# Column sums of w_out on VectorE instead of TensorE, with a new order of every engine's queue, in a clustered-attention and feed-forward kernel

## The chip, the cores and the metric

The kernel runs on one core of one Trainium2 chip. The metric is the device time of one execution in microseconds (us); the time before is the median of 3 runs, 220.64 us (220.5 to 221.01).

## The reference

Clustered attention (4 batches, 8 heads, 768 tokens, head dimension 64, 16 clusters) is followed by a feed-forward layer with a SoLU, a layer norm without bias and a second product (3072 tokens, d_model 512, d_ff 1024). All inputs and the output are float32.

```python
q_assign = argmax(q_n @ c_n.T); k_assign = argmax(k_n @ c_n.T)      # normalised rows, 16 clusters
scores = scale * q @ k.T, kept where q_assign == k_assign, else -1e9
x = softmax(scores) @ v                                              # -> (3072, 512)
h = x @ w_in
solu = h * exp(h - max(h)) / sum(exp(h - max(h)))
ln = (solu - mean(solu)) / sqrt(var(solu) + 1e-6) * g_ln
out = ln @ w_out
```

## The kernel before, in words

**The work.** The attention is cut into 96 units of 256 queries against 768 keys (24 per batch). The scores of all units are one long row of columns, cut into 144 regions of 1024. For region r, `S{r}.0` and `S{r}.1` are TensorE products into one of two PSUM tiles `sb` (L644), `E{r}` is the exponential on ScalarE (L654), and `V{n}.0`, `V{n}.1` are the products of unit n with the values, into the PSUM tile `ob` (L666). Units are put in groups; in batch 0 group g is units 2g and 2g+1. `N{g}` on VectorE divides the group by its sums (a reciprocal, L678, and a product, L689) and so empties `ob`: the first V of group g+1 needs N{g} (L1154 to L1158). Batch 0 has regions S0 to S35.

**Its operands.** In batches 1 to 3 the loads `ld` (L412, four pieces of 192 KB for two pairs of heads, read in runs of 32 floats, 128 bytes) fill the tiles `raw`; `xt` (L420, VectorE) transposes them; `ca` (L436 to L440) casts them, mostly on GpSimd, into `qbig` and `kbig`; `cl` (L469, TensorE) multiplies with the cluster centres, and `tb`, `mx`, `oh`, `ot` (VectorE) and `pl` (L541) turn that into cluster rows of `qbig` and `kbig`. `lv` (L558) loads the values, `cv` casts them. `ld1.0.0` is the q and `ld1.0.1` the k of batch 1's first two pairs, `ld1.2.0` the q of the next two. `cl1.0` needs `xt1.0.0` and `xt1.0.1`.

**The feed-forward part.** Row tiles of 128 tokens, f = 0 to 23, run in between: `h` (L777), `hm`, `ex`, `u`, `tu`, `bn`, `y` (L849), `sc`, `ou`. The layer norm's mean is folded into the weights: `w_out_c` is g·w_out less the mean of g·w_out over d_ff. `lo0` to `lo3` load w_out, two blocks of 128 rows each, into `w_g` (L599, 512 KB); `li0` and `li1` load w_in with a cast to bfloat16 from GpSimd's queue (L583). `gk` keeps -g as `g_ln2`. `gw` (L595, GpSimd) spreads g/d_ff over 32 columns in `g_wide`; `me0` and `me1` (L605, TensorE) sum the columns of w_out with it in eight float32 products, each of which is two instructions in the profile, 32 rows of PSUM to each product of four; `mk` (L614, VectorE) copies the sums out; `mf` (L617, two instructions) adds the four strips with the constant matrix `fold` and spreads the mean to 128 rows; `km` (L614) copies it out; `ce0` to `ce7` (L621 on VectorE, L625 with L627 on GpSimd) make `w_out_c`. `y0.0` needs `ce0` and `ce1`.

**What sets the order.** Every step is a named entry; `ORDER` lists all of them by hand, and each engine runs its own in that order, each waiting for what it reads. `AWAY` moves a step to another engine. SyncE's (SP's) queue issues nearly all loads, and one hardware queue (q1 in the profile) serves them. GpSimd's loads are on a software queue (q0). Both use the same 16 DMA engines.

Of the kernel before, what the change touches and what calls it, by code (L numbers as in the profile page):

```python
# [38 lines left out]
lc ld0.0.0.0 ld0.0.1.0 ld0.0.0 ld0.0.1 wu ld0.1.0 ld0.1.1 ld0.2.0 cx cy lv0.0 ld0.2.1 tp0.0.0.0 cz  # L39
ld0.3.0 tp0.0.0.1 xa0.0.0 lg tp0.0.1.0 xt0.0.0 ca0.0.0.0.0 lv0.1 cp lo1 ca0.0.0.0.1 cb tp0.0.1.1  # L40
xa0.0.1 ld0.3.1 ca0.0.0.1.0 ca0.0.1.0.0 cl0.0 cc lo2 xt0.0.1 ca0.0.0.1.1 tp0.1.0.0 tb0.0
ca0.0.1.1.0 tp0.1.0.1 mx0.0 xa0.1.0 cl0.0.1 ca0.0.1.0.1 oh0.0 xt0.1.0 tp0.1.1.0 ca0.0.1.1.1 tb0.0.1
ld1.0.0.0 tp0.1.1.1 xa0.1.1 ca0.1.0.0 mx0.0.1 ot0.0 ld1.0.0.1 xt0.1.1 tp0.2.0.0 oh0.0.1 pl0.0.1.1
tp0.2.0.1 xa0.2.0 ot0.0.1 cl0.1 z1 pl0.0.1.0 pl0.0.0.1 pl0.0.0.0 cv0.0.0 pl0.0.1.1.0 xt0.2.0 S0.0
pl0.0.1.0.1 S0.1 pl0.0.1.1.1 tb0.1 tp0.2.1.0 pl0.0.1.0.0 E0 S1.0 xa0.2.1 tp0.2.1.1 ca0.1.0.1 S1.1
xt0.2.1 cv0.0.1 tp0.3.0.0 ca0.2.0.0 S2.0 E1 mx0.1 S2.1 cl0.2 z4 oh0.1 ca0.2.1.0 E2 xa0.3.0 S3.0
S3.1 ot0.1 V0.0 tp0.3.0.1 E3 ca0.1.1.0 S4.0 S4.1 xt0.3.0 V0.1 ca0.2.1.1 V1.0 E4 V1.1 tb0.2 S5.0 lo0
S5.1 z2 pl0.1.1.1 N0 tp0.3.1.0 E5 S6.0 pl0.1.1.0 xa0.3.1 S6.1 V2.0 lo3 V2.1 mx0.2 pl0.1.0.1 E6
tp0.3.1.1 ld1.0.0.2 pl0.1.0.0 S7.0 ca0.1.1.1 gt xt0.3.1 S7.1 lv0.2 cv0.1.1 V3.0 V3.1 gk oh0.2 S8.0
# [2 lines left out]
pl0.2.1.1 V6.0 V6.1 oh0.3 ca0.3.0.1 S12.0 S12.1 ca0.3.1.0 V7.0 S13.0 E12 ld1.0.1.1 S13.1 ot0.3
ca0.3.1.1 cv0.2.0 me1 E13 pl0.3.0.0 S14.0 pl0.3.1.0 cv0.2.1 lv0.3 S14.1 mk V7.1 E14 pl0.3.1.1 S15.0
N3 S15.1 mf z3 ld1.0.1.2 pl0.3.0.1 E15 ld1.0.1 S16.0 km S16.1 V8.0 V8.1 E16 li0 S17.0 ce2 S17.1
V9.0 V9.1 E17 S18.0 N4 S18.1 li1 ld1.2.0.0 E18 S19.0 S19.1 cv0.3.0 cv0.3.1 xt1.0.0 ld1.2.0.1 E19
V10.0 V10.1 ce1 V11.0 V11.1 S20.0 N5 S20.1 S21.0 E20 S21.1 V12.0 V12.1 xt1.0.1 E21 V13.0 S22.0
S22.1 ce3 ca1.0.1.0 V13.1 E22 S23.0 N6 S23.1 cl1.0 xt1.1.0 E23 ce0 S24.0 S24.1 ptx0 xt1.1.1 V14.0
V14.1 E24 V15.0 S25.0 S25.1 tx0 V15.1 E25 z5 ca1.1.0.0 S26.0 N7 S26.1 cl1.1 ce5 E26 tb1.1 S27.0
S27.1 tb1.0 V16.0 V16.1 E27 S28.0 mx1.0 S28.1 V17.0 V17.1 ld1.2.0.2 E28 ca1.0.0.0 S29.0 N8 S29.1
h0.0.0 oh1.0 E29 V18.0 ld1.2.0 S30.0 S30.1 h0.0.1 ot1.0 E30 S31.0 S31.1 ld1.2.1.0 V18.1 ce4 V19.0  # L60
E31 pl1.0.0.0 V19.1 S32.0 S32.1 N9 h0.1.0 ld1.2.1.1 E32 hm0.0 S33.0 pl1.0.1.1 S33.1 V20.0 h0.1.1
E33 ld1.2.1.2 pl1.0.1.0 S34.0 S34.1 V20.1 V21.0 E34 V21.1 pl1.0.0.1 S35.0 ld1.2.1 N10 S35.1 h1.0.0
E35 ca1.0.1.1 hm0.1 S36.0 S36.1 lv1.0 V22.0 xt1.2.0 h1.0.1 bl1.0 E36 S37.0 S37.1 hm1.0 ca1.0.0.1
V22.1 tx2 V23.0 E37 V23.1 S38.0 N11 S38.1 ca1.1.1.0 h1.1.0 E38 lv1.1 S39.0 ca1.2.0.0 S39.1 h1.1.1
tx4 E39 xt1.2.1 S40.0 ca1.1.1.1 S40.1 E40 hm1.1 cl1.2 xt1.3.0 cv1.0.0 ex0.0 S41.0 S41.1 cv1.0.1
V24.0 V24.1 tb1.2 V25.0 V25.1 E41 V26.0 u0.0 S42.0 V26.1 S42.1 N12 h2.0.0 E42 h2.0.1 xt1.3.1 V27.0
h2.1.0 ex1.0 ce6 tu0 S43.0 hm2.0 S43.1 h2.1.1 E43 V27.1 S44.0 hm2.1 ld2.0.0.0 S44.1 h3.0.0 E44
ld2.0.0.1 bn0.0 cl1.3 u1.0 bn0.1 lv1.2 ex2.0 V28.0 V28.1 tb1.3 S45.0 V29.0 V29.1 mx1.2 ld2.0.0.2
S45.1 h3.0.1 ca1.2.1.0 E45 ld2.0.0 S46.0 S46.1 oh1.2 h3.1.0 ca1.3.0.1 E46 y0.0 N13 h3.1.1 cv1.1.1
S47.0 S47.1 bn1.0 ca1.1.0.1 cv1.1.0 ld2.0.1.0 y0.1 E47 hm3.0 S48.0 S48.1 y0.2 ot1.2 E48 tu1 V30.0  # L70
S49.0 S49.1 ce7 V30.1 V31.0 E49 V31.1 ld2.0.1.1 S50.0 as0 as1 ca1.2.0.1 pl1.2.0.1 bn1.1 S50.1
h4.0.0 ld2.0.1.2 E50 hm3.1 S51.0 pl1.2.1.1 S51.1 V32.0 ag0 V32.1 E51 y0.3 pl1.2.1.0 N14 S52.0 S52.1
h4.0.1 ld2.0.1 pl1.2.0.0 al0 E52 S53.0 as2 S53.1 bl1.2 V33.0 u2.0 V33.1 E53 h4.1.0 lv1.3 hm4.0
h4.1.1 ag1 ex3.0 V34.0 S54.0 xt2.0.0 ld2.2.0.0 S54.1 S55.0 S55.1 ld2.2.0.1 ca1.2.1.1 V34.1 E54 sc0
V35.0 h5.0.0 u3.0 h5.0.1 hm4.1 E55 S56.0 S56.1 bn2.0 y1.0 E56 bn2.1 S57.0 ld2.2.0.2 S57.1 V35.1
hm5.0 y1.1 cv1.2.0 ca2.0.0.1 y1.2 E57 N15 tu2 S58.0 ca2.0.0.0 S58.1 xt2.0.1 h5.1.0 E58 al1 S59.0
S59.1 ou0 xt2.1.0 V36.0 ca1.3.1.0 V36.1 ld2.2.0 V37.0 V37.1 E59 V38.0 ld2.2.1.0 cv1.2.1 ag2 S60.0
S60.1 ca1.3.0.0 xt2.1.1 h5.1.1 E60 V38.1 y1.3 as3 hm5.1 cv1.3.0 S61.0 ex4.0 S61.1 ca1.3.1.1 S62.0
bn3.0 ld2.2.1.1 S62.1 cl2.1 N16 al2 E61 cl2.0 u4.0 bn3.1 tu3 E62 sc1 V39.0 V39.1 S63.0 tb2.1 S63.1
# [1279 lines left out]
```

## Time and profile before

| | |
|---|---|
| median of 3 runs | 220.64 us |
| profiled execution, first to last instruction | 224.4 us |
| TensorE (PE) busy | 213.4 us, 95% |
| ScalarE (ACT) busy | 190.0 us, 85% |
| VectorE (DVE) busy | 182.4 us, 81% |
| GpSimd (POOL) busy | 162.3 us, 72% |
| mean granted TensorE clock | 0.992 |

The profile is of one execution of its own. It gives a span of 224.4 us, 3.8 us over the median of the timed runs, and no other time of its own; differences worked out in the profile are taken over to the median as they are. In a timeline row the numbers are start, duration, engine, line, operation, tiles and shape, with the idle time before it and what ended that in brackets. A row of stretches gives the busy time of each engine in the stretch (instructions in parentheses), then the granted clock, the mean busy share of the DMA engines and GB/s. SPq is SyncE's issuing of a DMA.

### The profile page before, as it was taken

To read this page: it belongs to the slowest core of one execution; us is meant where nothing else is said; L and a number is where in the kernel's file an instruction comes from. 1 tells how busy PE (TensorE), PEld (TensorE's weight loads), DVE (VectorE), ACT (ScalarE), POOL (GpSimd) and SP (SyncE) were. 2 spreads that over 40 slices of the span, in tenths; PEclk is the share of its full clock that TensorE was granted. 3 is DMA by queue.
4 is the path that set the end of the run, shared out by engine and by line. 5 is a ranking of instruction groups with operands and counts; after the bars stand their busy time and mean duration, and the time that the engine had idled before them with its cause. 6 is when DMAs were issued, how large, how long until landed. Compare 5 with 4: busy or idle time off the path is not lost.

```text
span 224.4 us, 6272 instructions
## 1 busy us (share of the span) xinstructions
PE 213.4 (95%) x2400; PEld 149.4 (67%) x2431; DVE 182.4 (81%) x431; ACT 190.0 (85%) x239; POOL 162.3 (72%) x202
## 2 busy tenths in 40 slices
...
GB/s 212 386 350 225 171 179 201 170 174 104 50 75 179 149 184 212 181 214 177 216 147 275 164 157 102 169 116 173 113 209 96 94 34 165 133 167 128 189 61 142
DMA packets 120878, 37.28 MB, mean 166 GB/s; under 512 B 109960, under 2 KB 116368, under 8 KB 120848
## 3 DMA queue, kind: packets, MB, share of 16 engines
...
HBM read 23.11 MB, written 6.29 MB: 131 GB/s over the span
## 4 chain that ended last, share of the span: by engine, by line
PE 81%; POOL 8%; DMA 4%; DVE 2%; issue 2%; SPq 0%; DVEq 0%; POOLq 0%
PE sb L644 24%; PE hb L777 17%; PE mb L849 16%; PE ob L666 13%; PE hb L469 5%; DMA raw<-in_k_dram 4%; POOL kbig L440 2%; POOL qbig L438 2%; PE hb L849 2%; PE sb L952 1%; POOL kbig L541 1%; POOL v L566 1%; POOL qbig L541 1%; PE hb L395 1%; DVE cst L483 0%
## 5 line engine op out<-in xcount | busy, mean ns | idle before, releaser
L654 ACT ACTIVATE e<-sb 128x1024 bf16<-128x1024 f32 x144 | 140.0, 1022 | 16.5 <-PE sb L644 15.2
L644 PE MATMUL sb<-qbig,kbig 80*128 80x256 bf16 (+3 forms) x648 | 85.3, 262 | 0.7 <-ACT e L654 0.3
L644 PEld LDWEIGHTS <-kbig 80*128 80x128 bf16 (+1 forms) x648 | 62.4, 120 | 25.3 <-issue 8.2
L810 POOL TENSOR_TENSOR u<-e_sb,w_st 128x1024 bf16<-128x1024 bf16 x21 | 45.1, 2147 | 18.7 <-ACT e_sb L803 12.3
L666 PEld LDWEIGHTS <-e 128*128 128x128 bf16 x1152 | 48.8, 98 | 12.3 <-issue 1.9
L666 PE MATMUL ob<-v,e 128*128 128x65 bf16 x1140 | 51.9, 193 | 0.4 <-DVE x L689 0.2
L777 PE MATMUL hb<-w_in_sb,xT 128*128 128x512 bf16 x172 | 50.4, 379 | 0.6
L849 PE MATMUL mb<-w_out_c,uT 128*128 128x512 bf16 x157 | 43.6, 379 | 0.6
L821 DVE BATCH_NORM_STATS2 bs<-u 128x6 f32<-128x512 bf16 x48 | 31.8, 681 | 1.1 <-POOL u L810 1.1
L803 ACT ACTIVATE e_sb<-w_st,nmax 128x1024 bf16<-128x1024 f32 (+1 forms) x25 | 27.9, 1114 | 5.5 <-DVE w_st L787 4.1
L440 POOL TENSOR_SCALAR kbig<-xt 64x768 bf16<-64x768 f32 (+1 forms) x30 | 27.4, 916 | 6.8 <-DVE xt L420 5.3
L438 POOL CAST qbig<-xt 64x768 bf16<-64x768 f32 (+1 forms) x32 | 26.7, 837 | 5.8 <-DVE xt L420 2.1
L420 DVE STREAM_TRANSPOSE xt<-raw 128x768 f32<-128x768 f32 x24 | 22.6, 961 | 5.3 <-DMA raw<-in_k_dram 5.2
L845 POOL TENSOR_TENSOR alpha<-var,halves 128x1 f32<-128x1 f32 x24 | 15.8, 659 | 11.8 <-DVE var L828 11.2
L849 PEld LDWEIGHTS <-uT 128*128 128x128 bf16 x176 | 15.2, 97 | 9.6
L777 PEld LDWEIGHTS <-xT 128*128 128x128 bf16 x192 | 16.1, 98 | 7.9
L787 DVE TENSOR_SCALAR_CACHE_REDUCE w_st<-hb,nmax 128x512 f32<-128x512 f32 x24 | 17.8, 743 | 3.2 <-PE hb L777 2.6
L689 DVE TENSOR_TENSOR x<-ob,den 128x256 bf16<-128x256 f32 (+2 forms) x40 | 19.0, 474 | 1.4
L787 DVE TENSOR_SCALAR_CACHE_REDUCE w_st<-hb 128x512 f32<-128x512 f32 x24 | 16.3, 679 | 4.1 <-PE hb L777 4.1
L678 DVE RECIPROCAL den<-ob 128x4 f32<-128x4 f32 (+2 forms) x40 | 7.2, 180 | 10.1 <-PE ob L666 9.6
L469 PE MATMUL hb<-xt,c_bd 128*32 128x384 f32 x96 | 11.4, 522 | 3.3 <-DVE xt L420 3.3
L541 POOL COPY qbig<-oht 32x768 f32<-32x768 f32 (+2 forms) x11 | 9.1, 824 | 6.5 <-DVE oht L508 3.3
...
## 6 DMA issues: line engine op xcount, KB each, us to landing
...
```

Of the source, the lines that this page charges most:

```text
L438: (nc.vector if e == "DVE" else nc.gpsimd).tensor_copy(dst, src)
L440: (nc.vector if e == "DVE" else nc.gpsimd).tensor_scalar(dst, src, scalar1=inv_C, scalar2=1.0, op0=Alu.mult, op1=Alu.mult)
L469: nc.tensor.matmul(bank_of(t, n)[c * NB:(c + 1) * NB, :L], w, xts[b, p, i][:, c0 + x * L:c0 + (x + 1) * L] .rearrange("p (n q) -> p q n", ...
L644: nc.tensor.matmul(reg[:, c:c + wd], kb[u, pp, side_of(h), keys], qb[u, pp, side_of(h), su * P:su * P + wd])
L654: nc.scalar.activation(es[r][:, :w], src, Act.Exp, scale=exp_scale, bias=-exp_scale)
L666: nc.tensor.matmul(ops_of(group_of[n])[:, s, :VW], es[r][:, c0:c0 + P], v1[index[b, pair_of(h)] % R][:, side_of(h), kt, :VW], start=(kt == ...
L777: nc.tensor.matmul(hb[f2][:], xTs[f][:, dc, :], w_in_sb[:, dc, f2 * BANK:(f2 + 1) * BANK], start=(dc == 0), stop=(dc == n_dc - 1))
L787: nc.vector.tensor_scalar(ff[f, "h"][:, f2 * BANK:(f2 + 1) * BANK], hb[f2][:], scalar1=-1.0, scalar2=nmax[:, f2 - 1:f2] if f2 else 3.0e38, ...
L803: nc.scalar.activation(ff[f, "e"][:, cols(f, f2)], ff[f, "h"][:, cols(f, f2)], Act.Exp, bias=ff[f, "nmax"][:, n_ff2 - 1:], scale=-1.0, acc ...
L810: (nc.vector if e == "DVE" else nc.gpsimd).tensor_tensor(ff[f, "u"][:, cols(f, f2)], ff[f, "e"][:, cols(f, f2)], ff[f, "h"][:, cols(f, f2) ...
L821: nc.vector.bn_stats(ff[f, "bs"][:, f2, :], ff[f, "u"][:, f2 * BANK:(f2 + 1) * BANK])
L849: nc.tensor.matmul(y_of(f, x), ff[f, "uT"][:, fc, :], w_out_c[:, fc, parts_of(f, x)], start=(fc == 0), stop=(fc == n_fc - 1))
```

## The change

- `me0` to `me7` are now VectorE operations, one for each block of 128 rows of w_out: the first multiplies block 0 with -g into the float32 tile `part`, the others multiply block fc with -g and add it to `part`. `me{fc}` needs `lo{fc // 2}`. `gw` and `mk` are gone, and `mf` sums `part` over all 128 rows with a `fold` of 1/d_ff.
- `cc` (which fills `c_bd`) is now needed only by the `cl` of batches 1 to 3, and the first `h` and `ptx0` no longer wait for `mk` or `km`.
- `ORDER` is another for every engine. SP now issues `lo2` alone early; `lo0` stands between the pieces of `ld1.0.1`, `lo3` and `lo1` behind it.
- In the new `ORDER`, `me2` stands ahead of `N5` on VectorE, and `N5` ahead of `V12.0` on TensorE; `cl1.0` stands ahead of `S22.0` (before: ahead of `S24.0`). `mf` stands behind `E34`, `km` behind `E35` (before: behind `S15` and `S16.0`).

```diff
@@ AWAY, to DVE
-    ce2 ce4 cv0.3.0 km mk pl0.0.0.0 pl0.1.0.0 pl0.2.0.1 pl0.2.1.0 pl0.3.0.0 pl1.2.0.0 pl2.0.0.0
+    ce2 ce4 cv0.3.0 km pl0.0.0.0 pl0.1.0.0 pl0.2.0.1 pl0.2.1.0 pl0.3.0.0 pl1.2.0.0 pl2.0.0.0
...
@@ ORDER (one line of each)
-S10.1 tb0.3 V5.0 ld1.0.0 V5.1 E10 sg S11.0 pl0.2.1.0 ld1.0.1.0 ca0.2.0.1 S11.1 N2 me0 E11 mx0.3
+E19 li1 ld1.2.0 S20.0 xt1.1.0 V11.1 S20.1 cv0.3.1 E20 me2 S21.0 ld1.2.1.0 S21.1 z5 cl1.0 N5 E21
...
-    def widen_g():
-        nc.gpsimd.tensor_scalar(g_wide[:], g_ln2[:].unsqueeze(2).to_broadcast([P, n_fc, NB]),
-                                scalar1=1.0 / d_ff, scalar2=1.0, op0=Alu.mult, op1=Alu.mult)
...
-    def sum_w_out(x):
-        for c in range(4):
-            fc = 4 * x + c
-            nc.tensor.matmul(hb[1][c * NB:(c + 1) * NB, :], g_wide[:, fc, :], w_g[:, fc, :],
-                             start=(x == 0), stop=(x == n_fc // 4 - 1),
-                             tile_position=(0, c * NB))
+    def sum_w_out(fc):
+        if fc == 0:
+            wt["part"] = mo.tile([P, d_model], F32, name="y")
+            nc.vector.tensor_scalar(wt["part"][:], w_g[:, fc, :], scalar1=g_ln2[:, fc:fc + 1],
+                                    scalar2=None, op0=Alu.mult)
+            return
+        nc.vector.scalar_tensor_tensor(out=wt["part"][:], in0=w_g[:, fc, :],
+                                       scalar=g_ln2[:, fc:fc + 1], in1=wt["part"][:],
+                                       op0=Alu.mult, op1=Alu.add)
...
-                [f"{half}{b}.{p}.0", f"{half}{b}.{p}.1", "cb"]
+                [f"{half}{b}.{p}.0", f"{half}{b}.{p}.1", "cb" if early(b) else "cc"]
...
-            add("ptx0", "PE", 0.46, s, turn_x_first, nd + hb_free[1][-1:] + ["mk"], take="h1")
+            add("ptx0", "PE", 0.46, s, turn_x_first, nd + hb_free[1][-1:], take="h1")
...
-                    nd += hb_free[f2][-1:] + ["mk" if f2 else "km"]
+                    nd += hb_free[f2][-1:]
...
-    add("sg", "POOL", 0.26, 8, lambda: nc.gpsimd.memset(fold[:], 1.0 / NB), ["cp"])
-    for x in range(2):
-        add(f"me{x}", "PE", 0.9, 16 + x, (lambda x=x: sum_w_out(x)),
-            [f"lo{2 * x}", f"lo{2 * x + 1}", "gw"] + ([] if x else hb_free[1][-1:]),
-            ["me0"] if x else list(last_tp), take=None if x else "h1")
-    e = on("mk", "ACT")
-    add("mk", e, 0.55, 18, (lambda e=e: keep("part", 1, e)), ["me1"], give="h1")
-    add("mf", "PE", 0.87, 18, fold_sums, ["mk", "sg"] + hb_free[0][-1:], take="h0")
+    add("sg", "POOL", 0.26, 8, lambda: nc.gpsimd.memset(fold[:], 1.0 / d_ff), ["cp"])
+    for fc in range(n_fc):
+        add(f"me{fc}", "DVE", 0.66, 16 + fc, (lambda fc=fc: sum_w_out(fc)),
+            [f"lo{fc // 2}", "gk"] + ([f"me{fc - 1}"] if fc else []))
+    add("mf", "PE", 0.87, 18, fold_sums, [f"me{n_fc - 1}", "sg"] + hb_free[0][-1:], take="h0")
```

SP's queue before, from the load `lo2` on (the tile `raw_234` is `ld1.0.0`, `raw_508` is `ld1.0.1`, `raw_651` is `ld1.2.0`; `w_g` rows are `lo2`, then `lo0` and `lo3`; `lo1` stands further up):

```order
L599 DMA w_g_110<-in_moe_w_out_dram 128x2x512
L412 DMA raw_234<-in_q_dram 32x48x32 x2
L599 DMA w_g_110<-in_moe_w_out_dram 128x2x512 x2
L412 DMA raw_234<-in_q_dram 32x48x32
L558 DMA vf_424<-in_v_dram 128x2x384
L412 DMA raw_234<-in_q_dram 32x48x32
L412 DMA raw_508<-in_k_dram 32x48x32 x2
L558 DMA vf_574<-in_v_dram 128x2x384
L412 DMA raw_508<-in_k_dram 32x48x32 x2
L412 DMA raw_651<-in_q_dram 32x48x32 x4
```

The same queue now, from `lo2` on (`raw_229` is `ld1.0.0`, `raw_389` is `ld1.0.1`, `raw_555` is `ld1.2.0`; the `w_g` rows are `lo2`, `lo0`, `lo3`, `lo1`):

```order
L594 DMA w_g_110<-in_moe_w_out_dram 128x2x512
L411 DMA raw_229<-in_q_dram 32x48x32 x2
L557 DMA vf_349<-in_v_dram 128x2x384
L411 DMA raw_389<-in_k_dram 32x48x32
L594 DMA w_g_110<-in_moe_w_out_dram 128x2x512
L411 DMA raw_389<-in_k_dram 32x48x32
L557 DMA vf_455<-in_v_dram 128x2x384
L411 DMA raw_389<-in_k_dram 32x48x32 x2
L594 DMA w_g_110<-in_moe_w_out_dram 128x2x512
L411 DMA raw_555<-in_q_dram 32x48x32
L594 DMA w_g_110<-in_moe_w_out_dram 128x2x512
L411 DMA raw_555<-in_q_dram 32x48x32
```

All four pieces of `ld1.0.1` stood behind the four loads of w_out; now two of these stand behind them, and the last, `lo1`, also behind the first piece of `ld1.2.0`.

VectorE's queue before, from `N4` on, at the first operands of batch 1 (`N4`, a cast of values, `xt1.0.0`, `N5`, `xt1.0.1`, `ce3`, `N6`, `xt1.1.0` with `xt1.1.1`):

```order
L678 RECIPROCAL den<-ob 128x4 [waits PE_49]
L689 TENSOR_TENSOR x<-ob,den 128x2x2x64 [waits DVE_49]
L566 CAST v_3_105<-vf 128x6x64 [waits DMAHW1_49]
L420 STREAM_TRANSPOSE xt<-raw 128x768 [waits DMAHW6_49,DMAHW4_49,DMAHW0_49]
L678 RECIPROCAL den<-ob 128x4 [waits PE_49]
L689 TENSOR_TENSOR x<-ob,den 128x2x2x64 [waits DVE_49]
L420 STREAM_TRANSPOSE xt<-raw 128x768 [waits DMAHW3_49,DMAHW7_49,DMAHW2_49,DMAHW0_49]
L621 SCALAR_TENSOR_TENSOR w_out_c<-w_g,g_ln_111,y 128x512
L678 RECIPROCAL den<-ob 128x4 [waits PE_49]
L689 TENSOR_TENSOR x<-ob,den 128x2x2x64 [waits DVE_49]
L420 STREAM_TRANSPOSE xt<-raw 128x768 [waits Pool_49] x2
```

The same place now (a cast of values, `xt1.0.0`, `N4`, `me1`, `xt1.0.1`, `xt1.1.0`, `me2`, `N5`, `xt1.1.1`):

```order
L565 CAST v_3_105<-vf 128x6x64 [waits DMAHW7_49]
L419 STREAM_TRANSPOSE xt<-raw 128x768 [waits DMAHW6_49,DMAHW2_49,DMAHW1_49]
L676 RECIPROCAL den<-ob 128x4 [waits PE_49]
L687 TENSOR_TENSOR x<-ob,den 128x2x2x64 [waits DVE_49]
L603 SCALAR_TENSOR_TENSOR y<-w_g,g_ln_111,y 128x512
L419 STREAM_TRANSPOSE xt<-raw 128x768 [waits DMAHW4_49,DMAHW6_49,DMAHW1_49,DMAHW0_49]
L419 STREAM_TRANSPOSE xt<-raw 128x768
L603 SCALAR_TENSOR_TENSOR y<-w_g,g_ln_111,y 128x512 [waits DMAHW4_49,DVE_49]
L676 RECIPROCAL den<-ob 128x4 [waits PE_49]
L687 TENSOR_TENSOR x<-ob,den 128x2x2x64 [waits DVE_49]
L419 STREAM_TRANSPOSE xt<-raw 128x768 [waits Pool_49]
```

`N5` stood ahead of the transpose that waits for `ld1.0.1`; it now stands behind that transpose and behind `me2`, which waits for a load of its own, `lo1`.

More of the change, by code (lines that the diff above doesn't have):

```diff
@@ L38 @@
 ORDER = """
[L39 to L49, printed above, removed]
```

198 lines of the change are left out of this document (103 added, 95 removed).

## The prediction

> **What bounds the kernel now.** The page and the table of stretches come first. The four stretches from 30 to 50 us are cut at the hole that the chain of waits shows; the last three are the rest of the span.
>
> ```profile
> span 224.4 us, 6272 instructions
> core 0: us, PE busy (x) PEld busy (x) DVE busy (x) ACT busy (x) POOL busy (x), PEclk, DMA share, GB/s
> 30.00:37.00 7.00, 6.54 (x96) 4.70 (x92) 3.13 (x8) 6.92 (x8) 4.46 (x6) 1.00 1.15 214
> 37.00:40.40 3.40, 0.13 (x4) 0.06 (x4) 1.09 (x2) 0.54 (x1) 0.02 (x1) 1.00 1.25 205
> 40.40:43.80 3.40, 3.40 (x23) 1.91 (x24) 2.89 (x6) 0.90 (x1) 3.32 (x5) 0.50 0.96 153
> 43.80:50.00 6.20, 6.03 (x88) 4.37 (x87) 4.76 (x10) 5.15 (x7) 3.38 (x4) 1.00 0.95 180
> ...
> 60.00:130.00 70.00, 69.35 (x850) 51.64 (x863) 63.19 (x134) 67.86 (x85) 58.71 (x62) 1.00 1.01 177
> 130.00:200.00 70.00, 69.26 (x798) 49.55 (x811) 56.32 (x140) 62.93 (x80) 48.40 (x51) 1.00 0.66 131
> 200.00:224.40 24.40, 20.56 (x144) 11.13 (x142) 19.26 (x53) 13.10 (x22) 11.04 (x13) 1.00 0.46 135
> ```
>
> From 60 to 200 us TensorE is busy 138.6 of 140 us. So from the end of the hole on, the time is the TensorE work still to be done, and a late restart, or work left over at the restart, goes to the end in full. The hole is 37.0 to 40.4 us: TensorE does 0.13 us of work in it, and the next 3.4 us run at half clock. TensorE's and VectorE's timelines say what ends it.
>
> ```profile
> 34.90 0.60 PE L644 MATMUL sb<-qbig,kbig 80*128 80x256 bf16 x4
> ...
> 36.20 0.87 PE L469 MATMUL hb<-xt,c_bd 128*32 128x384 f32 x4
> 40.34 1.50 PE L469 MATMUL hb<-xt,c_bd 128*32 128x384 f32 x4 [3.27 <-DVE xt L420]
> ...
> 28.04 0.17 DVE L678 RECIPROCAL den<-ob 128x4 f32<-128x4 f32 x1
> 28.25 0.43 DVE L689 TENSOR_TENSOR x<-ob,den 128x256 bf16<-128x256 f32 x1
> ...
> 39.31 0.98 DVE L420 STREAM_TRANSPOSE xt<-raw 128x768 f32<-128x768 f32 x1 [5.25 <-DMA raw<-in_k_dram]
> ```
>
> The first row is S22. `cl1.0` is half done when it waits for `xt1.0.1`, and that waits for the last piece of `ld1.0.1`, to 39.31 us. ScalarE runs dry meanwhile:
>
> ```profile
> 27.84 9.70 ACT L654 ACTIVATE e<-sb 128x1024 bf16<-128x1024 f32 x10 [0.22 <-PE sb L644]
> 42.90 1.02 ACT L654 ACTIVATE e<-sb 128x1024 bf16<-128x1024 f32 x1 [5.37 <-PE sb L644]
> 44.85 15.47 ACT L654 ACTIVATE e<-sb 128x1024 bf16<-128x1024 f32 x16 [0.93 <-PE sb L644]
> ```
>
> The ten end with E23, E24 starts at 42.90 and E25 at 44.85. Why does 192 KB land so late? First, each with its own landing time, the second and third pieces of `ld1.0.1`, the first piece of `ld1.2.0`, `li0` and `li1`; then both DMA queues from 34 to 38 us.
>
> ```profile
> L412 SPq DMA_DIRECT2D raw<-in_k_dram x1: 2446/2446/2446, 24.5 to 24.5; - x1
> DMA to landing us min/median/max: 5.9/5.9/5.9
> ...
> L412 SPq DMA_DIRECT2D raw<-in_k_dram x1: 467/467/467, 29.2 to 29.2; - x1
> DMA to landing us min/median/max: 4.2/4.2/4.2
> ...
> L412 SPq DMA_DIRECT2D raw<-in_q_dram x1: 2162/2162/2162, 30.5 to 30.5; - x1
> DMA to landing us min/median/max: 10.9/10.9/10.9
> ...
> L583 POOL DMA_DIRECT2D w_in_sb<-in_moe_w_in_dram x1: 960/960/960, 30.5 to 30.5; - x1
> DMA to landing us min/median/max: 6.6/6.6/6.6
> ...
> L583 POOL DMA_DIRECT2D w_in_sb<-in_moe_w_in_dram x1: 724/724/724, 31.4 to 31.4; - x1
> DMA to landing us min/median/max: 8.6/8.6/8.6
> ...
> q0 software_dynamic: 393, 0.77, 106.5%
> q1 hardware_dynamic: 244, 0.03, 10.0%
> ```
>
> The second piece lands at 30.4 us, the third at 33.4, the next two only at about 39 and 41.4, because w_in, issued at 30.5 us, takes the engines: in four microseconds its queue moves 0.77 MB and SP's 0.03 MB. The Trainium skill's page "DMA: Bandwidth & Descriptors" (Queues, rings and completion order) states that an engine goes round its queues packet by packet; the trace agrees as far as small packets behind large ones get few bytes.
>
> **Part by part: what is removed.** The sums on TensorE, their copy and the spreading of g:
>
> ```profile
> L605 PE MATMUL hb<-w_g,g_wide 128*32 128x512 f32 x16 | 2.1, 605 | 0.0
> L614 DVE COPY y<-hb 128x512 f32<-128x512 f32 x2 | 1.4, 692 | 0.7 <-PE hb L617 0.7
> L617 PE MATMUL hb<-y,fold 128*128 128x512 f32 x2 | 1.1, 632 | 0.0
> L621 DVE SCALAR_TENSOR_TENSOR w_out_c<-w_g,g_ln,y 128x512 bf16<-128x512 f32 x4 | 3.0, 757 | 0.0
> ```
>
> The sixteen take 2.1 us of TensorE, one copy 0.69 us of VectorE. All of it stands ahead of the hole, and who comes early to a hole waits longer. I cost it at nothing; if the hole were gone, TensorE's 2.1 us would count in full.
>
> **Added.** Eight operations like L621 (0.757 us; same elements, a bfloat16 output there), 6.1 us less the copy, 5.4 us of VectorE. `me0` and `me1` stand ahead of the hole, `me2` in it. `me3` to `me7` come after, 3.8 us; between 60 and 130 us VectorE has 6.8 of 70 us free, so they can be hidden, but not all at once. I take 0 us, with 2 us as the upper end (VectorE or GpSimd late by half of that work, since three GpSimd `ce` also move to where GpSimd is busy 58.7 of 70 us).
>
> **Moved: the loads.** Two prices are needed. A large load runs at the 386 GB/s of the page's second slice, before the small runs begin: 512 KB (524 thousand bytes) in 1.4 us, 384 KB in 1.0.
>
> ```profile
> GB/s 212 386 350 225 171 179 201 170 174 104 50 75 179 149 184 212 181 214 177 216 147 275 164 157 102 169 116 173 113 209 96 94 34 165 133 167 128 189 61 142
> ```
>
> A piece of 192 KB in runs of 128 bytes is 1536 packets: 1.1 us at the rate of SP's queue from 42 to 46 us (first row below), and 2.0 by the landings, since from 30.4 to 33.4 us one piece and one 384 KB load of values came in. I take the middle, 1.55.
>
> ```profile
> q1 hardware_dynamic: 5696, 0.72, 113.1%
> ...
> q0 software_dynamic: 2, 0.00, 2.7%
> ```
>
> (The second row is w_in's queue from 31 to 33 us: it has hardly begun.) Without w_in the last piece of `ld1.0.1` was due at 33.4 + 1.55 = 34.95; it now gets ahead of two of the 512 KB loads, and lands at 34.95 - 2.8 = 32.2, ahead of w_in's packets. That wait is then over.
>
> What is late next is `lo1`. On SP's queue it now stands behind exactly what before stood ahead of, and with, the first piece of `ld1.2.0`: the same set of transfers, in another order, on the same engines. That set was complete at 30.5 + 10.9 = 41.4 us. If w_in is issued at about the same time, 41.4 us is when `lo1` lands. GpSimd's queue holds the same steps ahead of w_in as before, less `gw`.
>
> On VectorE `me2` waits for `lo1`, and behind it are queued `N5`, `xt1.1.1`, `me3`, `N6`. TensorE waits for `N5` at `V12.0`, with S22 done; ScalarE then has nothing after E22. So: 41.4 + 0.76 (`me2`) + 0.64 (`N5`, 28.04 to 28.68 for an equal one) = 42.8 us for TensorE's restart, against 40.34 before: **+2.5 us**. Both restarts are at half clock, at the same price.
>
> **Work left over at the restart.** By the queues, before had done V12, V13, S23, `mf` and half of `cl1.0` when it restarted; now the four V and two S products and `mf` are still to do, and `cl1.0` is done. Prices from the chain of waits:
>
> ```profile
> 44.32 0.44 PE sb L644 x4
> 45.38 0.85 PE hb L469 x8
> 50.55 0.55 PE ob L666 x18
> ```
>
> V: 24 products at 0.55/18, 0.73 us; S23 0.44; `mf` 1.10 (L617); less half a `cl`, 0.42. Sum **+1.85 us**. Together 4.3 us: 224.4 goes to 228.7, the median 220.64 to **224.9**.
>
> A lower bound by ScalarE's pace: at half clock V12, V13 and S23 take 2.3 us, so E23 starts at 45.1 and E25 at 47.1, against 44.85: +2.2, 222.8. The rest of the new order can gain little: from 60 us on TensorE is idle 1.4 us and then 3.8 in the tail, mostly behind its last product. If `lo1` lands at 38 us, caught by part of w_in only, it is 3.4 less than 4.3: 221.5. With the 2 us above, this case reaches from 221.5 to 226.9.
>
> **The rivals.** *`lo1` escapes (faster).* If w_in's packets come after `lo1`, the set is complete at 33.4 plus two pieces: 36.5 us (35.6 to 37.4). `N5` ends at 37.9, the restart is 2.45 us earlier, the work left over still 1.85: -0.6. TensorE's hole is then from 35.3 (S22 done, at 34.90 + 0.44, if it comes when it did) to 37.9. If the clock stays up over so short a hole, half of 3.4 us more is saved: -2.3. I take -1.4, 219.2. It decides at w_in's issue: its packets began 2.5 us after it, at 33 us, so GpSimd would have to issue 3 us later than before, after 33.5. For it speaks that GpSimd waits in its queue for VectorE and TensorE, which have another order; against it, that it has less to do.
>
> The Trainium skill's page "TensorE: Matmul & The Clock Gate" (Part 1) states that the clock halves after an idle window of about 3.4 us. Before, 3.27 us of idleness were followed by 3.4 us at 0.50, so the trace agrees roughly; by that rule a hole of 2.6 us is likely spared.
>
> *The hole vanishes (faster).* With `lo1` ahead of 33.9 us TensorE goes on at 35.3: 5.0 us earlier, less 1.85, and 1.7 of clock: -4.85, 215.8. SP's queue would have to be some 2.6 us faster than by its rates above.
>
> *`lo1` half caught (no change).* Landing near 37.1 us, restart at 38.5: 220.6.
>
> *VectorE and GpSimd over-full (slower).* The late `me` and `ce` push `N`, `hm` and the casts back, and TensorE waits outside the hole: 2 us on top, 226.9. It decides if VectorE has no idle time between 43 and 60 us; before, it was busy 4.76 of 6.20 us at the start of that stretch.
>
> **How the numbers follow.** The forecast, with landings of `lo1` between 38 and 42 us, has 0.56; over-full engines 0.14; `lo1` escapes 0.17; the hole vanishes 0.05; half caught 0.08. A measurement of this kernel can tell 0.2%, 0.44 us, from no change. Faster 0.22, same 0.08, slower 0.70. The range is 218.5 to 227.0: it leaves out the vanished hole, the fast end of the escape and the slow end of the over-full case, about 0.15. The forecast's own range is 221.5 to 226.9.
>
> **What would show it.** VectorE's second in-place SCALAR_TENSOR_TENSOR waits for a DMA of `w_g` to about 41 us; the reciprocal behind it starts near 42; TensorE has a hole from about 35 to 42.8 that VectorE's x ends; E23 starts near 45. `xt1.0.1` runs near 33 us. Wrong would be a landing of `lo1` before w_in's two, a hole under 3 us, or, with the hole as said, a TensorE that is idle much less after it than before.

## The result and the profile after

The changed kernel takes 233.28 us (median of 4 runs, 231.7 to 234.78), the kernel before beside it 220.58 (220.5 to 221.01): a ratio of 1.0552 (95% interval 1.0466 to 1.0639), 12.7 us slower. The forecast was 224.9 us, 4.3 slower. The direction was right, the size three times the forecast, and the time lies above the range (227.0).

The times of the changed kernel and of its variants scatter by 2 to 10 us from run to run, those of the kernel before by 1.5; the ratios leave out runs more than 1.5% above the fastest of their kernel (in run 5 four of six), the medians keep them.

The page of the changed kernel, and what TensorE waited for in it:

```profile
span 233.0 us, 6274 instructions
...
PE 217.4 (93%) x2415; PEld 150.8 (65%) x2415; DVE 190.8 (82%) x438; ACT 191.0 (82%) x239; POOL 159.7 (69%) x201
...
PEclk9999985599999999999999999999999999999999
...
engine line waited for: us in total, times, longest us
PE ob L664 <- DVE x L687: 5.3, 3, 2.9
PE hb L775 <- DVE cst L482: 2.0, 1, 2.0
```

Two of the waits for x stand close together, and TensorE's timeline and VectorE's show them (line 603 is `me1` to `me7`, lines 676 and 687 are `N`, 565 is `cv0.3.0`, 419 is `xt`):

```profile
32.90 0.49 PE L664 MATMUL ob<-v,e 128*128 128x65 bf16 x6 [2.25 <-DVE x L687]
42.22 1.48 PE L664 MATMUL ob<-v,e 128*128 128x65 bf16 x24 [2.88 <-DVE x L687]
...
31.07 0.36 DVE L565 CAST v<-vf 128x384 bf16<-128x384 f32 x1 [2.27 <-DMA vf<-in_v_dram]
31.35 0.97 DVE L419 STREAM_TRANSPOSE xt<-raw 128x768 f32<-128x768 f32 x1
32.24 0.14 DVE L676 RECIPROCAL den<-ob 128x4 f32<-128x4 f32 x1
32.42 0.42 DVE L687 TENSOR_TENSOR x<-ob,den 128x256 bf16<-128x256 f32 x1
...
33.42 1.83 DVE L419 STREAM_TRANSPOSE xt<-raw 128x768 f32<-128x768 f32 x2
40.86 0.75 DVE L603 SCALAR_TENSOR_TENSOR y<-w_g,g_ln,y 128x512 f32<-128x512 f32 x1 [5.61 <-DMA w_g<-in_moe_w_out_dram]
41.53 0.18 DVE L676 RECIPROCAL den<-ob 128x4 f32<-128x4 f32 x1
```

The second hole is the forecast one: `me2` waits for `lo1` until 40.86 us, `N5` is queued behind it, and TensorE restarts at 42.22 (forecast: 41.4 and 42.8). It begins at 39.3 us, where the forecast had 35. The first was not forecast: `N4` is queued behind `cv0.3.0`, which waits for a load of values until 31.07 us, and behind `xt1.0.0`. TensorE runs at half clock from 33 to 46 us, in both stretches of work around the second hole. A third hole comes much later, at 121 us: VectorE's `sc4` waits for the buffer of the store `ou2`, and `tb2.3`, queued behind it, is what TensorE needs to have its accumulator free:

```profile
118.89 0.58 DVE L482 STREAM_TRANSPOSE cst<-hb 128x384 f32<-128x384 f32 x1 [0.51 <-PE hb L468]
121.75 0.75 DVE L862 TENSOR_SCALAR y<-mb,alpha 128x512 f32<-128x512 f32 x1 [2.28 <-DMA out_dram<-y]
122.42 0.57 DVE L482 STREAM_TRANSPOSE cst<-hb 128x384 f32<-128x384 f32 x1
...
123.04 0.59 PE L775 MATMUL hb<-w_in_sb,xT 128*128 128x512 bf16 x2 [1.97 <-DVE cst L482]
```

Against the first profile of before (one hole of 3.3 us, 3.4 us of work at half clock) the three holes are 3.8 us more, and 10.6 us of work at half clock instead of 3.4 cost 3.6 more: most of the 8.6 us between 224.4 and 233.0. But the timed runs are 12.7 us apart. That gap was the first thing to settle.

### The profile page after: what moved, and what is told of

It is laid out like the page before. It is cut to its first block, busy times and chain, and to the rows that moved or that the text cites. A ratio compares the mean times of both kernels' runs of the same rounds, so it can differ in the third digit from the quotient of the medians.

```text
span 233.0 us, 6274 instructions
## 1 busy us (share of the span) xinstructions
PE 217.4 (93%) x2415; PEld 150.8 (65%) x2415; DVE 190.8 (82%) x438; ACT 191.0 (82%) x239; POOL 159.7 (69%) x201
## 4 chain that ended last, share of the span: by engine, by line
PE 62%; DVE 14%; DMA 10%; POOL 5%; SPq 4%; issue 2%; ACT 0%; DVEq 0%; POOLq 0%; ACTq 0%
PE sb L642 18%; PE hb L775 14%; PE mb L847 13%; PE ob L664 10%; DMA w_g<-in_moe_w_out_dram 4%; DMA out_dram<-y 2%; PE hb L468 2%; DMA raw<-in_q_dram 2%; DMA xT<-x 2%; DVE x L687 2%; DVE xt L419 2%; SPq L594 2%; SPq L411 2%; DVE w_out_c L619 1%; PE hb L847 1%
## 5 line engine op out<-in xcount | busy, mean ns | idle before, releaser
L642 PE MATMUL sb<-qbig,kbig 80*128 80x256 bf16 (+3 forms) x648 | 93.8, 267 | 1.5 <-ACT e L652 1.0
L664 PEld LDWEIGHTS <-e 128*128 128x128 bf16 x1152 | 52.6, 99 | 18.0 <-issue 6.9
L664 PE MATMUL ob<-v,e 128*128 128x65 bf16 x1140 | 56.0, 196 | 5.4 <-DVE x L687 5.3
L775 PE MATMUL hb<-w_in_sb,xT 128*128 128x512 bf16 x192 | 54.5, 379 | 3.1 <-DVE cst L482 2.0
L847 PE MATMUL mb<-w_out_c,uT 128*128 128x512 bf16 x168 | 46.1, 379 | 0.0
L439 POOL TENSOR_SCALAR kbig<-xt 64x768 bf16<-64x768 f32 (+1 forms) x30 | 25.7, 858 | 11.0 <-DVE xt L419 9.3
L437 POOL CAST qbig<-xt 64x768 bf16<-64x768 f32 (+1 forms) x32 | 27.6, 867 | 4.2 <-ACT xt L405 3.1
L847 PEld LDWEIGHTS <-uT 128*128 128x128 bf16 x176 | 15.6, 97 | 10.9 <-issue 0.2
L843 POOL TENSOR_TENSOR alpha<-var,halves 128x1 f32<-128x1 f32 x24 | 13.1, 550 | 12.2 <-DVE var L826 10.2
L540 POOL COPY kbig<-oht 32x768 f32<-32x768 f32 (+2 forms) x17 | 11.6, 682 | 9.9 <-DVE oht L507 8.9
L860 ACT ACTIVATE y<-mb,alpha 128x512 f32<-128x512 f32 x12 | 8.3, 689 | 6.9 <-PE mb L847 5.0
L565 POOL CAST v<-vf 128x384 bf16<-128x384 f32 x21 | 12.3, 591 | 1.7 <-DMA vf<-in_v_dram 1.1
```

What stands on the lines that cost most here:

```text
L437: (nc.vector if e == "DVE" else nc.gpsimd).tensor_copy(dst, src)
L439: (nc.vector if e == "DVE" else nc.gpsimd).tensor_scalar(dst, src, scalar1=inv_C, scalar2=1.0, op0=Alu.mult, op1=Alu.mult)
L642: nc.tensor.matmul(reg[:, c:c + wd], kb[u, pp, side_of(h), keys], qb[u, pp, side_of(h), su * P:su * P + wd])
L664: nc.tensor.matmul(ops_of(group_of[n])[:, s, :VW], es[r][:, c0:c0 + P], v1[index[b, pair_of(h)] % R][:, side_of(h), kt, :VW], start=(kt == ...
L775: nc.tensor.matmul(hb[f2][:], xTs[f][:, dc, :], w_in_sb[:, dc, f2 * BANK:(f2 + 1) * BANK], start=(dc == 0), stop=(dc == n_dc - 1))
L847: nc.tensor.matmul(y_of(f, x), ff[f, "uT"][:, fc, :], w_out_c[:, fc, parts_of(f, x)], start=(fc == 0), stop=(fc == n_fc - 1))
```

## The experiments

**1. The kernel before, profiled again.** No edit.

> The kernel before, unchanged, profiled once more. Its first profile has a span of 224.4 us, its timed runs 220.6 us, which would be spans near 218.8. Theory: the hole at 37.0 to 40.4 us was longer in that one execution than it usually is; a second profile has a span of 218 to 220 us, and TensorE's hole there is 2 us or more shorter or gone, with a granted clock of 0.95 or more from 40 to 50 us. Rival: the hole belongs to the kernel; the span is again 223 to 225 us with the same hole, and the timed runs differ from a profiled one for another reason.

Measured: 220.28 us, span 218.5. Its page and ScalarE's timeline (the row at 37.49 is E24):

```profile
span 218.5 us, 6303 instructions
...
PE 212.4 (97%) x2431; PEld 147.8 (68%) x2431; DVE 182.5 (84%) x431; ACT 190.0 (87%) x239; POOL 161.1 (74%) x202
...
PEclk9999999999999999999999999999999999999999
...
37.49 1.02 ACT L654 ACTIVATE e<-sb 128x1024 bf16<-128x1024 f32 x1 [0.19 <-PE sb L644]
```

The theory holds: the hole at 37.0 to 40.4 us, from which the whole forecast started, is not there. The clock is full throughout, and E24 starts 5.4 us earlier than the 42.90 of the first profile. What differs is a race between two queues. SP's issues of the last two pieces of `ld1.0.1`, in the first profile and in this one, and the first issue of w_in here:

```profile
L412 SPq DMA_DIRECT2D raw<-in_k_dram x2: 467/552/638, 29.2 to 29.8; - x2
...
L412 SPq DMA_DIRECT2D raw<-in_k_dram x2: 466/554/642, 27.0 to 27.6; - x2
...
L583 POOL DMA_DIRECT2D w_in_sb<-in_moe_w_in_dram x1: 960/960/960, 31.8 to 31.8; - x1
```

The last piece was issued at 29.8 us there, 0.7 us ahead of w_in's issue at 30.5, and was caught behind it until 39.3; here it is issued at 27.6, 4.2 us ahead of w_in, and `xt1.0.1` runs at 33.51 without waiting for it. The first profile was of an unusual execution. Every timed run here is about 1.8 us longer than its span (220.28 and 218.5 in this one), so a span of 224.4 stands for 226.2 us, 5.6 over the median, and none of the 39 other timed runs of this kernel is above 221.67 us. So the span to compare with is 218.5. The profiled run of the changed kernel took 234.78 us, and its span, 233.0, is 14.5 us over that: 9.5 more of TensorE idle (15.6 against 6.1) and 5.0 more of it busy, which the half clock from 33 to 46 us explains (10.6 us of work at half clock, 5.3 more), though the 2.1 us of products saved should have taken off some of that.

**2. The sums behind N5 and N6.** One edit in VectorE's steps:

```diff
-N4 me1 xt1.0.1 xt1.1.0 me2 N5 xt1.1.1 me3 N6 me4 me5 tx0 N7 tb1.0 me6 tb1.1 mx1.0 N8 oh1.0 ot1.0 hm0.0
+N4 me1 xt1.0.1 xt1.1.0 N5 xt1.1.1 N6 tx0 me2 me3 N7 me4 tb1.0 tb1.1 me5 mx1.0 N8 oh1.0 ot1.0 hm0.0 me6
```

> The changed kernel with its sums me2 to me6 moved behind N5, N6 and the following steps in VectorE's queue, so that no normalisation stands behind a sum that waits for a piece of w_out. Theory (the wait of me2 is what holds TensorE until 42.2 us): TensorE restarts near 39.3 us, and 3 to 5 us are gained: 228.3 to 230.3 us, from 233.28. Rival (VectorE simply has too much work, the wait only moves it): less than 1 us is gained, 232.3 to 233.5.

Measured: 233.41 us (233.11 to 235.4), ratio 1.0601 (1.0554 to 1.0648). The hole ahead of 42 us is gone, and another has taken its place. TensorE's row, and GpSimd's:

```profile
54.86 1.48 PE L642 MATMUL sb<-qbig,kbig 80*128 80x256 bf16 x6 [4.46 <-POOL kbig L540]
...
44.59 0.50 POOL L565 CAST v<-vf 128x384 bf16<-128x384 f32 x1 [8.37 <-DMA vf<-in_v_dram]
45.18 2.85 POOL L439 TENSOR_SCALAR kbig<-xt 64x768 bf16<-64x768 f32 x3
```

GpSimd stands 8.4 us at `cv1.0.1` for a load of values, with five casts of batch 1 queued behind it; the cluster rows (line 540) behind those are what TensorE needs next. Up to E30 ScalarE is as far as in the kernel before (0.15 us behind), so the wait is gone; what was gained is lost again behind it. The theory's mechanism is right and its price wrong: the time fits the rival, but not for the rival's reason. GpSimd's queue has the same fault as VectorE's, a step that waits for a late load ahead of urgent ones; in the profile of the changed kernel TensorE stands only 0.4 us for `kbig`.

**3. N4 ahead of the cast that waits.**

```diff
-me0 pl0.3.0.0 cv0.3.0 xt1.0.0 N4 me1
+me0 pl0.3.0.0 N4 cv0.3.0 xt1.0.0 me1
```

> The changed kernel with N4 ahead of cv0.3.0 and xt1.0.0 in VectorE's queue, so that N4 does not wait for the load of values that lands at 31.05 us. Theory (the two holes are in a row, and what the first one gives back is lost again ahead of the second, which ends when lo1 has landed): the hole at 30.7 to 32.9 us goes, TensorE stands longer ahead of 42 us, and the time gains 0 to 1 us: 232.3 to 233.3. Rival (each hole is paid in full, with its stretch at half clock): 3.5 to 5 us are gained, 228.3 to 229.8.

Measured: 232.11 us (228.91 to 239.32), ratio 1.0439 (1.0364 to 1.0514). The hole at 33 us is gone and the next one is longer, 5.46 us ahead of 40.26 where it was 2.88. The profile is as the theory has it: what the first of two holes gives back is lost ahead of the second. The times scatter too widely to tell 0 to 1 us from 2, so the price is not shown.

**4. The store ou2 early** (SP's steps).

```diff
-tx6 lv2.2
+tx6 ou2 lv2.2
...
-ld3.2.0.1 ou2 ld3.2.0.2
+ld3.2.0.1 ld3.2.0.2
```

> The changed kernel with the store ou2 issued behind tx6, ahead of the raw pieces of the last batch, where before it stood in that region too. Theory (sc4 on VectorE waits for that store's buffer at 119.5 to 121.7 us, and tb2.3 behind it holds TensorE for 2.0 us): that hole goes and 1.5 to 2.5 us are gained, 230.8 to 231.8. Rival (TensorE waits there for VectorE's or SP's work in any case): less than 0.5 us, 232.8 to 233.5.

Measured: 233.2 us, with runs from 227.69 to 236.29, too scattered for an interval. In its profile no wait for cst is left, and TensorE stands 1.0 us for a uT at 125 us instead of 2.0. So the store is what `sc4` waited for; the gain cannot be read from these times.

**5. The sums alone, in the order of before.** Loads as before; in VectorE's steps:

```diff
-mk N3 km ce2 N4 cv0.3.0 xt1.0.0 N5 xt1.0.1 ce3 N6 xt1.1.0 xt1.1.1 tx0 N7
+me0 N3 me1 me2 N4 cv0.3.0 xt1.0.0 N5 xt1.0.1 me3 N6 xt1.1.0 xt1.1.1 me4 tx0 N7 me5
...
-oh1.0 ot1.0 ce4 N9 hm0.0 N10 hm0.1 xt1.2.0 hm1.0 N11
+oh1.0 ot1.0 me7 N9 hm0.0 km N10 ce3 hm0.1 xt1.2.0 hm1.0 ce2 N11 ce4
```

> The order of the kernel before, with every load in its old place; only the sums go to VectorE as in the changed kernel (me0 to me7 from the places of mk, km, ce2 and ce3 on to ot1.0, mf behind hm0.0, the eight ce behind it from 45 us on). This is the first part of the change alone. Theory (the loss comes from late loads and the new order; the sums themselves find room on VectorE): TensorE saves the 2.1 us of sixteen products in a stretch where it was fully busy, and the time is between 217.5 and 220.6 us. Rival (VectorE is over-full by 5.4 us of added work, and TensorE waits for it): 222 to 226 us, with TensorE waiting for x or cst of VectorE between 27 and 60 us.

Measured: 230.4 us (226.68 to 231.78), ratio 1.0342 (1.0278 to 1.0406). Both theories missed. TensorE waits 0.8 us for VectorE in all; its two long waits, ahead of 55.4 and 60.9 us, are for GpSimd's casts (qbig and v, 1.6 us each). VectorE has absorbed the sums; but the last sum ends at 44.7 us, so the mean exists at 47.9, and GpSimd's `ce`, 2 us each, now stand between casts. In the kernel before they filled idle time. Hence the next run.

**6. Late centring alone.** The kernel before, sums on TensorE, no work added to VectorE; `mf`, `km` and six `ce` later. In GpSimd's steps:

```diff
-li0 li1 cv0.3.1 ce1 ca1.0.1.0 ce0 z5 ca1.1.0.0 ce5 ca1.0.0.0 pl1.0.0.0 pl1.0.1.1 pl1.0.1.0 pl1.0.0.1 ca1.0.1.1 bl1.0 ca1.0.0.1 ca1.1.1.0
+li0 li1 cv0.3.1 ca1.0.1.0 z5 ca1.1.0.0 ca1.0.0.0 pl1.0.0.0 pl1.0.1.1 pl1.0.1.0 ce1 pl1.0.0.1 ce0 ca1.0.1.1 bl1.0 ca1.0.0.1 ce5 ca1.1.1.0
```

> The kernel before, with its sixteen products and all loads in their old places; only mf, km and the centring steps ce0 to ce5 come as late as in the run with the sums alone on VectorE (mf behind hm0.0, the ce from about 47 us on). VectorE gets no added work. Theory (what costs is that the mean comes late, so that the eight ce, which filled GpSimd's and VectorE's idle time from 30 to 45 us, fall into the stretch from 47 to 60 us where both are needed for the next batch): 226 to 230 us, with ScalarE's pace 5 to 8 us behind that of the kernel before at E42. Rival (the 5.4 us of work added to VectorE are the loss): 220.3 to 222 us.

Measured: 230.48 us (230.06 to 230.68), ratio 1.0443 (1.0427 to 1.0459). The theory holds, and above its upper end. The stretches 30 to 45 and 45 to 60 us, first in the kernel before (second profile), then here:

```profile
30.00:45.00 15.00, 14.52 (x220) 10.80 (x218) 12.79 (x24) 14.19 (x16) 11.10 (x14) 1.00 1.11 175
45.00:60.00 15.00, 15.00 (x192) 10.79 (x188) 11.40 (x28) 14.97 (x18) 13.25 (x16) 1.00 0.63 125
...
30.00:45.00 15.00, 14.35 (x214) 10.82 (x215) 10.93 (x21) 14.20 (x16) 5.02 (x9) 1.00 1.06 166
45.00:60.00 15.00, 11.78 (x119) 7.61 (x118) 11.72 (x22) 10.91 (x13) 13.59 (x15) 1.00 0.51 106
...
55.93 0.38 PE L643 MATMUL sb<-qbig,kbig 96*128 96x256 bf16 x2 [1.62 <-POOL qbig L437]
61.45 1.07 PE L665 MATMUL ob<-v,e 128*128 128x65 bf16 x30 [2.65 <-POOL v L565]
```

GpSimd (the fifth pair) does 6 us less in the first stretch and can do only 0.3 more in the second, since it was nearly full; its casts slip, and TensorE (the first pair) loses 3.2 us there. ScalarE's pace against the kernel before is +0.2 us at E30, +7.1 at E42, +10.1 at E60 and +10.3 from E66 to the end. So the lateness of the mean alone costs as much as run 5 does. The sums on VectorE, 5.4 us of added work, cost nothing beyond it that these runs can tell (230.4 with them, 230.48 without; the ratio with them is even the lower), but this is net of the 2.1 us of products on TensorE that run 5 saves and this run keeps.

**7. The sums close together.** As run 5, but with the mean early again:

```diff
-N3 me1 me2 N4 cv0.3.0 xt1.0.0 N5 xt1.0.1 me3 N6
+N3 me1 me2 me3 me4 N4 me5 me6 cv0.3.0 xt1.0.0 me7 N5 xt1.0.1 km N6
```

> The order of the kernel before with the sums on VectorE, as in the run with the sums alone, but the eight sums close together from 27 to 35 us, mf behind S21, and the ce from 36 us on, near their old places. Theory (the late mean is what costs, and it need not be late): 219 to 223 us; TensorE waits up to 2 us for x between 30 and 36 us. Rival (VectorE has no room for 5.4 us more before 60 us, wherever they stand): 226 us or more.

Measured: 224.59 us (223.66 to 226.11), ratio 1.0185 (1.014 to 1.0231), between the two forecasts. Early centring saves 6 us of the 10, but the sums now stand in the way of VectorE's own steps:

```profile
32.38 0.89 PE L664 MATMUL ob<-v,e 128*128 128x65 bf16 x24 [1.02 <-DVE x L687]
33.10 1.04 PE L642 MATMUL sb<-qbig,kbig 80*128 80x256 bf16 x8
35.92 1.12 PE L615 MATMUL hb<-y,fold 128*128 128x512 f32 x2 [1.78 <-DVE y L603]
```

**8. The same, with these two waits eased.**

```diff
-N3 me1 me2 me3 me4 N4 me5 me6 cv0.3.0 xt1.0.0 me7 N5 xt1.0.1 km N6
+N3 me1 me2 N4 me3 me4 cv0.3.0 xt1.0.0 me5 N5 me6 me7 xt1.0.1 N6 km
```

> The order of the kernel before with the sums on VectorE from 27 to 36 us as in the earlier run of that kind, but with two sums fewer ahead of N4, two behind N5, and mf as late as its accumulator allows, behind S23. In the earlier run TensorE stood 1.0 us for N4 and 1.8 us for the last sum, and the whole loss against the kernel before, 3.8 us, was there by E24 and stayed. Theory (with these waits gone the products saved show): 219.5 to 222 us. Rival (any place between 27 and 36 us holds up VectorE's steps for the next batch): 223.5 to 226 us.

Measured: 224.22 us (223.63 to 225.8), ratio 1.0173 (1.0142 to 1.0205). This is the rival's time: the waits come back one step on (1.3 us for the next `N`, 0.8 for `km`). TensorE's 2.1 us saved show only as 0.9 us of ScalarE's pace at E18 in run 7, 0.6 here. No version with the sums on VectorE came out ahead of the kernel before.

**9. w_in late** (GpSimd's steps).

```diff
-li0 li1 cv0.3.1 z5 ca1.1.1.1
+cv0.3.1 z5 ca1.1.1.1 li0 li1
```

> The changed kernel with the two loads of w_in issued on GpSimd behind ca1.1.1.1 (near 36 to 40 us) where they were issued at 31 us. Theory (w_in's megabyte takes the transfer engines from the loads that VectorE and GpSimd wait for): lo1 lands by 37 us, N5 is not held up, and 2 to 5 us are gained: 228 to 231 us; the first product of h waits for w_in until 46 to 49 us. Rival (w_in is not what delays lo1): lo1 lands at 40 us or later as before, and the time is 233 to 237 us.

Measured: 232.05 us (230.43 to 233.19), ratio 1.0509 (1.0468 to 1.055). w_in is now issued at 38.9 us, and `me2` runs at 35.39 after a wait of 1.88 us for w_g, 5.5 us earlier than in the changed kernel. This does not show by itself that w_in held up `lo1`, since SP also issued `lo1` 2.1 us earlier here (29.45 us against 31.53), and in run 2, with w_in in its old place, it landed as early. The landings of all profiles together do. First the issue and landing of `lo1` in the changed kernel, where w_in was issued at 31.15 us, then in run 2, where it was issued at 30.69:

```profile
L594 SPq DMA_DIRECT2D w_g<-in_moe_w_out_dram x1: 738/738/738, 31.5 to 31.5; - x1
DMA to landing us min/median/max: 9.2/9.2/9.2
...
L594 SPq DMA_DIRECT2D w_g<-in_moe_w_out_dram x1: 746/746/746, 29.6 to 29.6; - x1
DMA to landing us min/median/max: 5.5/5.5/5.5
```

Issued 0.9 us or more ahead of w_in, `lo1` takes 5.5 to 5.9 us (runs 2, 9, 11 and 12); issued 0.7 us or less ahead of it, or behind it, 7.4 to 11.9 us (the changed kernel, runs 3, 4, 10 and 13). Of the time at most 1 to 2 us are gained, less than the theory had and hardly more than the scatter, though E24 is 2.9 us late instead of 8.3: other waits take its place.

**10. The changed kernel again.** No edit.

> The changed kernel once more, unchanged, for a second profile and four more times, since its times scatter over 3 us and those of its variants over 10. Theory (holes set by landings that differ from execution to execution, and by half clock behind them): times between 228 and 239 us, a hole behind N4 or N5 of another length than 2.25 and 2.9 us. Rival (the holes are a property of the order, the same in each execution): both holes within 0.5 us of the first profile's.

Measured: 234.05 us (231.86 to 234.24), ratio 1.0583 (1.0542 to 1.0623). The order is the same and the holes are not: 1.1 us at 31 us (2.25 in the first profile), 6.25 ahead of 41.46 (2.88 ahead of 42.22), 1.6 at 122 us. `lo1` lands at 40.0 us. Only the restart, set by that landing, agrees to 0.8 us. The times kept closer together than the theory had it.

**11. Four waiting steps moved at once:** the edits of runs 2, 3 and 4, and `cv1.0.1` behind `pl1.0.1.0` on GpSimd.

> The changed kernel with four steps that wait for transfers moved behind the steps that TensorE needs: me2 to me6 behind N5 and N6, cv0.3.0 and xt1.0.0 behind N4, cv1.0.1 on GpSimd behind the casts of keys of batch 1 (in the run with me2 to me6 moved alone, GpSimd stood 8.4 us for the load of values lv1.0 with those casts behind it, and TensorE 4.5 us for them), and the store ou2 ahead of the last batch's loads. Theory (the loss is the sum of such queue waits): 221 to 226 us with a granted clock above 0.99. Rival (a new wait takes each one's place, because the transfers due from 33 to 45 us are too many in any order): 229 us or more.

Measured: 231.99 us (229.78 to 234.69), ratio 1.0476 (1.0416 to 1.0536). The time is the rival's. At E48 ScalarE is 3.0 us behind the kernel before (run 10: 8.9), at E54 it is 10.0 behind. In between TensorE stands 2.8 us for uT, ahead of 71.0, and goes on at half clock.

**12. The changed kernel without seven of its eight sums.** In `sum_w_out`:

```diff
+        if fc:
+            return
```

> The changed kernel with me1 to me7 left out, so that the mean is formed of the first of eight chunks alone; all else, the loads of w_out and the place of mf and of the ce included, stays. Theory (the wait for lo1 ahead of N5 is the larger half of the loss, the order behind it and the late ce the other): the hole behind N5 goes, the one behind N4 stays or not by the landing of lv0.3, and the time is 226 to 230 us. Rival (the loss is in the rest of the new order, whoever adds up w_out): 231 to 234 us.

Measured: 230.49 us (228.06 to 232.13), ratio 1.0471 (1.0413 to 1.0529), between the two forecasts. No wait for w_out is left (`lo1` landed at 35.4 us), and E24 and E30 are where the kernel before has them (within 0.1 us). Then TensorE waits 3.07 us for GpSimd's kbig.

**13. What is left of the new order:** run 12 with the mean and the `ce` early, and the moves of runs 3, 4 and 11.

> The changed kernel with me1 to me7 left out (the mean is formed of the first of eight chunks alone), mf at S20 and the ce from 35 us on as early as in the kernel before, and the three other moves of waiting steps (cv0.3.0 and xt1.0.0 behind N4, cv1.0.1 behind the casts of batch 1, ou2 ahead of the last batch's loads). What is left of the change is its order from 60 us on and its order of loads. Theory (the loss is made of the waits ahead of N4, N5 and the casts, and of the late ce; the rest of the order costs little): 219.5 to 223.5 us. Rival (the rest of the new order is worse by itself): 225 us or more, with TensorE standing in several places behind 60 us.

Measured: 227.94 us (225.95 to 231.45), ratio 1.0264 (1.0236 to 1.0291). The time is the rival's: 7.2 us by the medians, 5.8 by the ratio, remain with the rest of the new order, its order of loads included. But TensorE does not stand in several places behind 60 us. Two waits stand out, one on each side of it, and what ended the second is in SP's timeline, here and then in the kernel before (second profile):

```profile
51.81 0.86 PE L644 MATMUL sb<-qbig,kbig 80*128 80x256 bf16 x6 [2.79 <-POOL kbig L540]
71.03 0.60 PE L849 MATMUL mb<-w_out_c,uT 128*128 128x512 bf16 x2 [2.50 <-DMA uT<-u]
...
64.46 2.81 SPq L816 DMA_TRANSPOSE uT<-u  x1
...
57.92 1.23 SPq L816 DMA_TRANSPOSE uT<-u  x1
```

The first wait is GpSimd's: the new order has seven casts of batch 1 (`ca1`) ahead of the copies of cluster rows (`pl1.0`) and an eighth ahead of the last of these, where the order before has three. Ahead of the second, `tu0` stands behind six loads of values and keys on SP, and is issued 6.5 us later than before. In the changed kernel's own profile TensorE stands 0.4 us for `kbig` and not at all for uT: these two waits come to light when the earlier ones are gone.

## Why the prediction was right in sign and wrong in size

- **TensorE is the bound, and what it loses stays lost.** Right. In runs 6, 7 and 8 ScalarE's distance to the kernel before is constant to 0.1 us from E66 to the end.
- **`lo1` is late behind w_in; `me2`, `N5`, TensorE.** Right in the profiles of the changed kernel, in mechanism and time: `lo1` forecast at 41.4 us, seen at 40.8 and 40.0; restart forecast at 42.8, seen at 42.22 and 41.46; E25 forecast 2.2 us or more later, seen at 47.46 against 44.85, 2.6 later. Two of the prediction's own signs of being wrong came true in part. The hole, 2.88 us, is under the 3 us that it named, because the first hole and the half clock behind it had put back the end of S22 by 4 us; in run 10 it lasts 6.25. And `lo1` landed between w_in's two loads (39.7 and 43.1 us), not behind both. Like the wait of before, this is a race. The prediction had it decided by w_in's issue, which would have to come after 33.5 us; it is decided by the lead of `lo1`'s issue (run 9), and in run 2 `lo1` landed at 35.1 with w_in issued at 30.7. The kernel was no faster for it (233.41 us), so the right sign did not hang on this mechanism, and is in part luck.
- **"224.4 goes to 228.7, the median 220.64 to 224.9."** This step failed first. It takes a difference against the profiled execution over to the median, though that execution was 5.6 us slower than the timed ones (run 1). It had a hole that they do not have. From the usual E24, 37.49, to that of the changed kernel is 8.3 us:

```profile
45.82 1.02 ACT L652 ACTIVATE e<-sb 128x1024 bf16<-128x1024 f32 x1 [0.15 <-ACT e L652]
```

  Of these, 2.9 is what the forecast's two terms stood for (4.3) and 5.4 is the hole in its base. The table ahead of the prediction told it: 224.4 us beside 220.64.
- **The eight `me`: "I take 0 us, with 2 us as the upper end".** The work itself is free where it is spread out, net of the products saved: 230.4 us with the sums on VectorE and 230.48 without, both with late `ce`. Close together it is not: runs 7 and 8 lose 3.9 and 3.5 us to VectorE's own steps. The step that failed is what hangs on it. Eight sums in a chain, spread over VectorE's gaps, bring the mean late, and the `ce` leave idle time for a full stretch: 9.8 us in the order of before (run 6), where the upper end had 2. In the changed kernel's own order it is less: the early mean and three moves together gain 2.6 us by the medians, 4.6 by the ratios (runs 12 and 13). The rival "over-full" named the place and GpSimd's share, and took VectorE's idle time to decide; in run 6 GpSimd's was the one that counted.
- **"The rest of the new order can gain little."** Nothing was said of what it can lose; the sum had it at nothing. Run 13 puts it at 7.2 us: casts ahead of cluster rows on GpSimd, `tu` behind loads on SP; in the changed kernel itself also `N4` behind a cast and `sc4` behind a store. All of them stand in the two orders; the prediction worked out only the one hole.
- **The sum.** Taken away one after another in the changed kernel's own order, seven sums give 2.8 us (run 12), the early mean and three moves 2.6 more (run 13), and 7.2 are left: together 12.6 of the 12.7, by medians of runs that scatter by some us. Another order of taking them away may divide it otherwise, since waits in a row hide each other (runs 2, 3 and 9); the 9.8 of run 6, measured in the order of before, is no term of it. The exact shares stay open, as does why the half clock and the products saved do not quite add up to 5.0 us.
- **"By that rule a hole of 2.6 us is likely spared."** Wrong here: the hole of 2.25 us halved the clock (next section).
